# BigBird attention and a cosine router: turning, scores, values and row sums on 64x64 quarters of TensorE, with the router's logits taken along

## The chip, the cores and the metric

The kernel runs on one core of one Trainium2 chip. The metric is the device time of one execution in microseconds (us); less is better. The core has a matrix engine (TensorE, PE in the profile; its weight loads are listed as PEld), VectorE (DVE), ScalarE (ACT), GpSimd (POOL), and SyncE (SP), which issues most of the DMA transfers. Matrix products land in PSUM, which has eight banks of 512 float32 per partition; everything else is kept in SBUF.

## The reference

Block-sparse attention over 4 batches x 8 heads x 768 tokens x 64, followed by a mixture of 8 experts in which each token goes to one expert:

```python
scores = scale * np.matmul(q, k.transpose(0, 1, 3, 2))
scores = np.where(mask, scores, -1000000000.0)        # mask by blocks of 32 x 32
scores = scores - np.max(scores, axis=-1, keepdims=True)
attn = np.exp(scores)
attn = attn / (np.sum(attn, axis=-1, keepdims=True) + 1e-09)
out = np.matmul(attn, v)                              # then (B,H,S,D) -> x: (B*S, H*D)
...
xn = x / (np.linalg.norm(x, axis=-1, keepdims=True) + 1e-06)
en = expert_emb / (np.linalg.norm(expert_emb, axis=-1, keepdims=True) + 1e-06)
logits = xn @ en.T / tau
expert_idx = np.argmax(logits, axis=1)                # gate_w: the softmax there
h = np.maximum(x[mask] @ w1[e], 0.0)
out[mask] = gate_w[mask, None] * (h @ w2[e])
```

All inputs are float32.

## The kernel before

The attention (`attention_fast`, L527) goes over 16 pairs of heads. Of a pair, K and Q are loaded with tokens on partitions, three or so pairs ahead, and turned by TensorE so that the 2 x 64 head dimensions lie on the partitions (`turn_fast`, L248): four parts to a pair, each with three 128x128 transposes into one PSUM bank (L257) and one copy, of K by DVE (L261), of Q with the scale by ACT (L259).

The work of a pair is 12 units: two halves of the queries (384 each) times six chunks of 128 keys. `score_fast` (L264) makes the scores of a unit, keys on partitions, for both heads: first the mask, as a bf16 product of 24 block rows (L272; one product per head on 32 rows of the array), then K times Q with 64 rows of the array per head (L275), added onto it in PSUM; ACT takes the exponential of both heads at once (L278), without subtracting a maximum. `attend_fast` (L282) adds the unit's exponentials into `esum` on DVE (L291, L293) and multiplies them with V (L295): 128 rows of the array, 64 columns per head, added up in one PSUM bank over the six units of a half; after the sixth ACT copies the bank to `at` (L299).

`settle` (L303) finishes a half: three transposes bring `at` back to tokens on partitions (L313), six products of a column of ones sum `esum` over the keys (L317), and DVE divides (L320 to L323) and writes into `x`. After the eight halves of a batch, `route` squares the rows of `x` on ACT, takes the root on POOL (L354), transposes `x` again on TensorE, 24 times (L363), copies that on DVE (L365), and makes the logits with 48 matmuls of eight columns (L368). Then come some small DVE steps (L376 to L391) with the softmax and the argmax, and two products that rank the tokens within their expert (`rk`, L401 and L402). `dispatch` and `experts` follow when all four batches are routed. A second attention (`attention_exact`) stands in an If and isn't entered with these inputs.

Float32 products are two instructions each on TensorE (a load and a matmul twice); bf16 products and transposes are one. The loop of `attention_fast` (L545 to L557) gives the scores of the next unit, a part of a turn at four of the twelve units, the values of this unit, and settling one unit into the next half. Within that, the framework's scheduler sets the order of each engine's queue from its own plan, and the semaphores. PSUM: `big` has two buffers of two banks (scores, also the transposes of `x`), `acc` two of one bank (`av`), `small` two of one bank (turning, settling, logits, ranks).

Of the kernel before, what the change touches and what calls it, by code (L numbers as in the profile page):

```python
# [10 lines left out]
F32 = mybir.dt.float32  # L11
# [3 lines left out]
ALU = mybir.AluOpType  # L15
# [3 lines left out]
P = 128  # L19
# [22 lines left out]
class Net:  # L42
    pass

# [38 lines left out]
def build_mask(k):  # L83
# [39 lines left out]
    if not k.exact:  # L123
        k.kmask = k.const.tile([P, S], BF16, name="kmask")
        k.qmask = k.const.tile([P, S], BF16, name="qmask")
        for h in range(2):
            nc.vector.tensor_copy(out=k.kmask[32 * h:32 * h + NB, :], in_=krow)
            nc.scalar.copy(out=k.qmask[32 * h:32 * h + NB, :], in_=qr[0:NB, 0:S])
        return
# [10 lines left out]
def build_experts(k):  # L140
# [12 lines left out]
    tp = k.small.tile([P, 512], F32, name="tp", tag="small")  # L153
# [3 lines left out]
    nc.vector.tensor_copy(out=k.en, in_=tp[:, 0:ND * E].rearrange("p (c e) -> p c e", e=E))  # L157

# [67 lines left out]
def attend(k, u):  # L226
# [5 lines left out]
    if c == 0:  # L232
        k.av = k.small.tile([P, NC, D], F32, name="av", tag="small")
# [14 lines left out]
def turn_fast(k, g, part):  # L248

    nc = k.nc  # L250
    name, lo = ("k", "q")[part // 2], part % 2 * NQ
    if part == 0:
        k.turned[g] = {n: k.tp.tile([P, S], F32, name=f"{n}t", tag=f"{n}t") for n in ("k", "q")}
    src, dst = k.loaded[g]["kq".index(name)], k.turned[g][name]
    ps = k.small.tile([P, 512], F32, name="turn", tag="small")
    for c in range(NQ):
        nc.tensor.transpose(ps[:, c * P:(c + 1) * P], src[:, lo + c].rearrange("p h d -> p (h d)"), k.ident)  # L257
    if name == "q":
        nc.scalar.mul(out=dst[:, lo * P:lo * P + HALF], in_=ps[:, 0:HALF], mul=SCALE)  # L259
    else:  # L260
        nc.vector.tensor_copy(out=dst[:, lo * P:lo * P + HALF], in_=ps[:, 0:HALF])  # L261


def score_fast(k, u):  # L264
# [3 lines left out]
    kt, qt = k.turned[g]["k"], k.turned[g]["q"]  # L268
    ps = k.big.tile([P, 2, 512], F32, name="sc", tag="big")
    keys, queries = slice(kc * P, (kc + 1) * P), slice(qh * HALF, (qh + 1) * HALF)  # L270
# [11 lines left out]
def attend_fast(k, u):  # L282
# [3 lines left out]
    if kc == 0:  # L286
        k.av = k.acc.tile([P, 512], F32, name="av", tag="av")
# [6 lines left out]
    for h in range(2):  # L294
        nc.tensor.matmul(k.av[D * h:D * (h + 1), 0:HALF], lhsT=v[:, h, kc, :], rhs=e[:, h, :],  # L295
                         start=(kc == 0), stop=(kc == NC - 1))
    if kc == NC - 1:
        at = k.sp.tile([P, HALF], F32, name="at", tag="at")
        nc.scalar.copy(out=at, in_=k.av[:, 0:HALF])  # L299
        k.done[u // NC] = (at, k.esum)  # L300


def settle(k, w):  # L303
# [7 lines left out]
    ps = k.small.tile([P, 512], F32, name="back", tag="small")  # L311
# [8 lines left out]
    nc.vector.tensor_scalar(out=den, in0=ps[:, HALF:HALF + 2 * NQ], scalar1=1e-9, scalar2=None, op0=ALU.add)  # L320
    inv = k.sp.tile([P, NQ, 2], F32, name="inv", tag="inv")
    nc.vector.reciprocal(out=inv.rearrange("p t h -> p (t h)"), in_=den)
    nc.vector.tensor_tensor(  # L323
        out=k.x[b][:, qh * NQ:(qh + 1) * NQ, j * P:(j + 1) * P].rearrange("p t (h d) -> p t h d", h=2),
        in0=ps[:, 0:HALF].rearrange("p (t h d) -> p t h d", t=NQ, h=2),
        in1=inv.unsqueeze(3).broadcast_to([P, NQ, 2, D]), op=ALU.mult)


def count_good(k):
# [11 lines left out]
    ps = k.small.tile([P, 512], F32, name="good_ps", tag="small")  # L341
# [5 lines left out]
def route(k, b):  # L347
# [10 lines left out]
    lg = k.small.tile([P, NC, E], F32, name="lg", tag="small")  # L358
    for c2 in range(0, NC, 2):
        ps = k.big.tile([P, 2 * ND, P], F32, name="xt_ps", tag="big")  # L360
        for i in range(2 * ND):
            c, d = c2 + i // ND, i % ND
            nc.tensor.transpose(ps[:, i, :], x[:, c, d * P:(d + 1) * P], k.ident)  # L363
        xt = p.tile([P, 2 * ND, P], F32, name="xt")
        nc.vector.tensor_copy(out=xt, in_=ps)  # L365
        for c in (c2, c2 + 1):
            for d in range(ND):
                nc.tensor.matmul(lg[:, c, :], lhsT=xt[:, (c - c2) * ND + d, :], rhs=k.en[:, d, :],  # L368
                                 start=(d == 0), stop=(d == ND - 1))

# [156 lines left out]
def attention_fast(n, ctx):  # L527
# [14 lines left out]
    for part in range(4):  # L542
        turn_fast(n, 0, part)
    score_fast(n, 0)
    for u in range(units):  # L545
# [3 lines left out]
        if u + 1 < units:  # L549
            score_fast(n, u + 1)  # L550
# [136 lines left out]
```

## Time and profile before

| what | value |
|---|---|
| three runs | 997.63, 1002.25, 1003.86 us; median 1002.25 |
| profiled execution | 999.39 us, of which the span from its first to its last instruction is 997.6 |
| attention and routing | 20 to 547 us of the span |
| finding the slots, experts, tail | 547 to 998 us |
| granted clock of TensorE, mean over the span | 0.947 |

The profile records every instruction's start and duration on each engine, and what released it where it waited. Busy time on PE is the time in which at least one matmul is in the array, draining included; since matmuls overlap, the start of one group to the start of the next says more than the length of either. A load (PEld) belongs to a matmul and may run while an earlier matmul streams. The granted clock is a share of full speed, 1.00 for 2.4 GHz and 0.50 for 1.2 GHz.

### The profile page before, as it was taken

What the parts mean: (1) busy time and instruction counts of PE and PEld (TensorE: products, weight loads), DVE (VectorE), ACT (ScalarE), POOL (GpSimd) and SP (SyncE); (2) the same over time, 40 slices, a digit from 0 to 9 for tenths busy, and PEclk for the clock granted to TensorE, in tenths of its full rate; (3) what the DMA queues carried; (4) which work ended last, traced back from release to release, by engine and by line L of the source; (5) the groups of instructions that cost most, each with busy time, mean ns of one, the idle gap of its engine ahead of it and who ended that gap; (6) DMA issues with size and microseconds to landing.
All of it is one profiled execution on the core that took longest, in us unless ns stands there. A gap on an engine that the chain in (4) does not pass through costs nothing.

```text
span 997.6 us, 12554 instructions
## 1 busy us (share of the span) xinstructions
PE 942.3 (94%) x5230; PEld 542.6 (54%) x5230; DVE 298.0 (30%) x513; ACT 218.0 (22%) x340; POOL 73.1 (7%) x105
## 2 busy tenths in 40 slices
PE   5999999999999999999998489999999999999984
PEld 2344354344454434634446466766776776776662
DVE  2444443444434444334444511111111111111110
ACT  2434432433423444233342000000000000000000
POOL 1000000000010000100001100110110111111010
PEclk9999996999979999789996589999999999999997
DMA  7111112111221111020001299989889998998872
GB/s 174 30 34 49 48 32 80 48 44 37 48 79 33 48 49 32 17 79 1 1 1 42 102 400 407 401 311 342 306 314 329 311 326 316 330 321 314 289 280 77
DMA packets 105243, 161.69 MB, mean 162 GB/s; under 512 B 52620, under 2 KB 56716, under 8 KB 104662
## 3 DMA queue, kind: packets, MB, share of 16 engines
q1 hardware_dynamic: 100694, 146.84, 43.3%
q0 software_dynamic: 4480, 13.91, 3.5%
q8 instruction: 45, 0.74, 0.3%
q14 instruction: 24, 0.20, 0.1%
HBM read 148.14 MB, written 13.38 MB: 162 GB/s over the span
## 4 chain that ended last, share of the span: by engine, by line
PE 89%; issue 5%; DVE 2%; DMA 1%; SPq 1%; ACT 0%; POOL 0%; POOLq 0%; ACTq 0%
PE sc L275 18%; PE hp L510 18%; PE yp L518 17%; PE av L295 16%; PE sc L272 5%; PE back L317 4%; PE turn L257 3%; PE lg L368 3%; PE back L313 2%; PE xg_ps L501 1%; PE slot_ps L462 1%; PE xt_ps L363 1%; DMA out_dram<-y,slot 1%; SPq L173 1%; DVE xt L365 0%
## 5 line engine op out<-in xcount | busy, mean ns | idle before, releaser
L278 ACT ACTIVATE e<-sc 128x768 f32<-128x768 f32 x192 | 155.6, 810 | 287.3 <-PE sc L275 287.3
L510 PEld LDWEIGHTS hp<-xgt,w 128*128 128x128 f32 x1728 | 199.5, 192 | 25.4 <-issue 11.0
L510 PE MATMUL hp<-xgt,w 128*128 128x128 f32 x1728 | 204.2, 277 | 9.1 <-ACT h L513 4.9
L275 PE MATMUL sc<-qt,kt 64*128 64x384 f32 x768 | 192.4, 556 | 0.0
L518 PE MATMUL yp<-w,h 128*128 128x512 f32 x432 | 189.9, 592 | 0.0
L295 PE MATMUL av<-e,vld 128*64 128x384 f32 x768 | 173.1, 523 | 0.0
L293 DVE TENSOR_TENSOR esum<-esum,e 128x768 f32<-128x768 f32 x128 | 122.3, 956 | 105.9 <-ACT e L278 105.9
L518 PEld LDWEIGHTS yp<-w,h 128*128 128x128 f32 x432 | 80.0, 190 | 90.4 <-issue 90.4
L513 ACT ACTIVATE h<-hp 128x512 f32<-128x512 f32 x27 | 16.1, 597 | 412.7 <-PE hp L510 383.7
L295 PEld LDWEIGHTS av<-e,vld 128*64 128x64 f32 x768 | 39.2, 137 | 81.9 <-issue 63.4
L275 PEld LDWEIGHTS sc<-qt,kt 64*128 64x128 f32 x768 | 62.6, 191 | 35.9 <-issue 35.8
L272 PEld LDWEIGHTS <-kmask 24*128 24x128 bf16 x384 | 18.2, 91 | 102.3 <-issue 101.8
L520 DVE TENSOR_SCALAR y<-yp,xg 128x512 f32<-128x512 f32 x27 | 20.3, 750 | 158.6 <-PE yp L518 158.6
L514 DVE TENSOR_SCALAR h<-hp 128x512 f32<-128x512 f32 x27 | 18.7, 691 | 160.9 <-PE hp L510 160.9
L272 PE MATMUL sc<-qmask,kmask 24*128 24x384 bf16 x384 | 66.5, 340 | 0.0
L291 DVE TENSOR_TENSOR esum<-e 128x768 f32<-128x768 f32 x32 | 30.7, 958 | 110.6 <-ACT e L278 110.6
L521 POOL DMA_INDIRECT out_dram<-y,slot x27 | 27.5, 1017 | 352.9 <-DVE y L520 338.5
L317 PEld LDWEIGHTS back<-ones,esum 128*128 128x128 f32 x384 | 45.4, 192 | 0.0
L317 PE MATMUL back<-ones,esum 128*128 128x1 f32 x384 | 44.7, 243 | 0.0
L354 POOL TENSOR_TENSOR nrm<-nrm,half 128x6 f32<-128x6 f32 x4 | 5.3, 1330 | 485.3 <-ACT sq L353 485.3
L368 PEld LDWEIGHTS lg<-en,xt 128*128 128x128 f32 x192 | 29.4, 242 | 6.3 <-DVE xt L365 4.6
L486 POOL DMA_INDIRECT xg<-x_dram,slot x29 | 29.9, 1032 | 29.2 <-DVE slot L464 20.6
(124 smaller groups left out, 392.8 us busy)
## 6 DMA issues: line engine op xcount, KB each, us to landing
w<-in_moe_w_dram SPq DMA_DIRECT2D x58, 2048.0 KB, 9.4
x_dram<-x SPq DMA_DIRECT2D x4, 1539.0 KB, 6.1
kld<-in_k_dram SPq DMA_DIRECT2D x32, 192.0 KB, 3.0
qld<-in_q_dram SPq DMA_DIRECT2D x32, 192.0 KB, 3.2
vld<-in_v_dram SPq DMA_DIRECT2D x16, 384.0 KB, 3.2
xg<-x_dram,slot POOLq DMA_INDIRECT x29, 7.4
out_dram<-y,slot POOLq DMA_INDIRECT x27, 7.4
x_dram<-zero SPq DMA_DIRECT2D x1, 2.0 KB
```

Source lines behind the costliest of these rows:

```text
L257: nc.tensor.transpose(ps[:, c * P:(c + 1) * P], src[:, lo + c].rearrange("p h d -> p (h d)"), k.ident)
L272: nc.tensor.matmul(ps[:, h, 0:HALF], lhsT=k.kmask[32 * h:32 * h + NB, keys], rhs=k.qmask[32 * h:32 * h + NB, queries], start=True, stop=False)
L275: nc.tensor.matmul(ps[:, h, 0:HALF], lhsT=kt[D * h:D * (h + 1), keys], rhs=qt[D * h:D * (h + 1), queries], start=False, stop=True)
L278: nc.scalar.activation(e, ps[:, :, 0:HALF], ACT.Exp)
L291: nc.vector.tensor_tensor(out=k.esum, in0=k.first, in1=e, op=ALU.add)
L293: nc.vector.tensor_tensor(out=k.esum, in0=k.esum, in1=e, op=ALU.add)
L295: nc.tensor.matmul(k.av[D * h:D * (h + 1), 0:HALF], lhsT=v[:, h, kc, :], rhs=e[:, h, :], start=(kc == 0), stop=(kc == NC - 1))
L317: nc.tensor.matmul(ps[:, i:i + 1], lhsT=esum[:, h, t * P:(t + 1) * P], rhs=k.ones[:, 0:1], start=True, stop=True)
L368: nc.tensor.matmul(lg[:, c, :], lhsT=xt[:, (c - c2) * ND + d, :], rhs=k.en[:, d, :], start=(d == 0), stop=(d == ND - 1))
L486: nc.gpsimd.indirect_dma_start(out=x[:, :], out_offset=None, in_=k.x_dram[:, :], in_offset=bass.IndirectOffsetOnAxis(ap=k.slot[:, t:t + 1] ...
L510: nc.tensor.matmul(hp[:, f, :], lhsT=w1[:, d, f * P:(f + 1) * P], rhs=xt[:, d, :], start=(d == 0), stop=(d == ND - 1))
L518: nc.tensor.matmul(yp, lhsT=h[:, f, :], rhs=w2[:, f, :], start=(f == 0), stop=(f == NF - 1))
```

## The change

All products of the attention are cut so that each uses a 64x64 quarter of the array: 64 rows in, 64 columns out, and four such products, one for each quarter, follow one another. Products on different rows write different PSUM banks.

- The mask rows are padded from 24 to 64 per head with zeros (two fills on POOL). A unit's mask and scores are each four products: head by row half of the array, key half by column half.
- The values contract over 64 keys at a time, into two banks of `av`; `part` (ACT) copies one, and DVE adds the other to it to give `at`. `av` has one buffer of two banks instead of two of one.
- `turn_fast` has two parts instead of four, each for K and Q together: 24 products with the identity in place of transposes.
- `settle` turns `at` back with 12 products whose right side holds, beside the identity, the eight columns of the normalised expert embeddings for these 64 dimensions (`back`, built once in `build_experts`), and so gives each head's share of the logits; these go to `part`, and `route` sums them over the heads with one DVE step. The logits' transposes and products leave `route` (they stay for the exact path). The sums of `esum` are 24 products of one column.
- The loop gives scores two units ahead instead of one, settling before the values, and turning after them. `small` has one buffer of two banks instead of two of one.

```diff
+        nc.gpsimd.memset(k.kmask, 0.0)
+        nc.gpsimd.memset(k.qmask, 0.0)
...
+    k.back = k.const.tile([P, NPAIR, D + E], F32, name="back")
+    for h in range(2):
+        rows = slice(D * h, D * (h + 1))
+        nc.vector.tensor_copy(out=k.back[rows, :, 0:D],
+                              in_=k.ident[rows, rows].unsqueeze(1).broadcast_to([D, NPAIR, D]))
+        nc.vector.tensor_copy(out=k.back[rows, :, D:D + E], in_=k.en[rows])
...
 def turn_fast(k, g, part):
-    for c in range(NQ):
-        nc.tensor.transpose(ps[:, c * P:(c + 1) * P], src[:, lo + c].rearrange("p h d -> p (h d)"), k.ident)
+    for n in range(2):
+        src = k.loaded[g][n]
+        for c in range(NQ):
+            for r in range(2):
+                toks = slice(D * r, D * (r + 1))
+                for h in range(2):
+                    nc.tensor.matmul(ps[D * h:D * (h + 1), r, n, c, :], lhsT=src[toks, part * NQ + c, h, :],
+                                     rhs=k.ident[toks, toks], start=True, stop=True)
+    kt, qt = [t[:, chunks].rearrange("p c r t -> p r c t") for t in k.turned[g]]
+    nc.vector.tensor_copy(out=kt, in_=ps[:, :, 0])
+    nc.scalar.mul(out=qt, in_=ps[:, :, 1], mul=SCALE)
...
 def score_fast(k, u):
-    for h in range(2):
-        nc.tensor.matmul(ps[:, h, 0:HALF], lhsT=k.kmask[32 * h:32 * h + NB, keys],
-                         rhs=k.qmask[32 * h:32 * h + NB, queries], start=True, stop=False)
-    for h in range(2):
-        nc.tensor.matmul(ps[:, h, 0:HALF], lhsT=kt[D * h:D * (h + 1), keys], rhs=qt[D * h:D * (h + 1), queries],
-                         start=False, stop=True)
+    quarters = [(h, r, slice(kc * P + D * r, kc * P + D * (r + 1))) for r in range(2) for h in range(2)]
+    for rows, cols, first in ((k.kmask, k.qmask, True), (kt, qt, False)):
+        for h, r, keys in quarters:
+            nc.tensor.matmul(ps[D * r:D * (r + 1), h, 0:HALF], lhsT=rows[D * h:D * (h + 1), keys],
+                             rhs=cols[D * h:D * (h + 1), queries], start=first, stop=not first)
...
 def attend_fast(k, u):
-    for h in range(2):
-        nc.tensor.matmul(k.av[D * h:D * (h + 1), 0:HALF], lhsT=v[:, h, kc, :], rhs=e[:, h, :],
-                         start=(kc == 0), stop=(kc == NC - 1))
+    for r in range(2):
+        for h in range(2):
+            nc.tensor.matmul(k.av[D * h:D * (h + 1), r, 0:HALF], lhsT=v[D * r:D * (r + 1), h, kc, :],
+                             rhs=e[D * r:D * (r + 1), h, :], start=(kc == 0), stop=(kc == NC - 1))
     if kc == NC - 1:
+        part = k.sp.tile([P, HALF], F32, name="part", tag="part")
+        nc.scalar.copy(out=part, in_=k.av[:, 1, 0:HALF])
         at = k.sp.tile([P, HALF], F32, name="at", tag="at")
-        nc.scalar.copy(out=at, in_=k.av[:, 0:HALF])
+        nc.vector.tensor_tensor(out=at, in0=k.av[:, 0, 0:HALF], in1=part, op=ALU.add)
...
 def settle(k, w):
+    W = D + E
     for t in range(NQ):
-        nc.tensor.transpose(ps[:, t * P:(t + 1) * P], at[:, t * P:(t + 1) * P], k.ident)
-    for t in range(NQ):
         for h in range(2):
-            i = HALF + 2 * t + h
-            nc.tensor.matmul(ps[:, i:i + 1], lhsT=esum[:, h, t * P:(t + 1) * P], rhs=k.ones[:, 0:1],
-                             start=True, stop=True)
+            for s in range(2):
+                cols = slice(t * P + D * s, t * P + D * (s + 1))
+                nc.tensor.matmul(rows[D * s:D * (s + 1), t, h, :], lhsT=at[D * h:D * (h + 1), cols],
+                                 rhs=k.back[D * h:D * (h + 1), j, :], start=True, stop=True)
+    for t in range(NQ):
+        for h in range(2):
+            for r in range(2):
+                for s in range(2):
+                    cols = slice(t * P + D * s, t * P + D * (s + 1))
+                    nc.tensor.matmul(sums[D * s:D * (s + 1), t, h, r:r + 1], lhsT=esum[D * r:D * (r + 1), h, cols],
+                                     rhs=k.ones[D * r:D * (r + 1), 0:1], start=True, stop=True)
...
+    nc.vector.reduce_sum(out=den.rearrange("p (t h) -> p t h", t=NQ), in_=sums, axis=AX.X)
...
+    nc.vector.tensor_tensor(out=k.part[b][:, chunks, 2 * j:2 * j + 2, :], in0=rows[:, :, :, D:W],
+                            in1=inv.unsqueeze(3).broadcast_to([P, NQ, 2, E]), op=ALU.mult)
...
 def route(k, b):
+    lg = logits(k, x) if k.exact else l
+    if not k.exact:
+        nc.vector.reduce_sum(out=l, in_=k.part[b].rearrange("p c h e -> p c e h"), axis=AX.X)
...
 def attention_fast(n, ctx):
-    n.big, n.acc = pool("big_f", 2, space=PSUM), pool("acc", 2, space=PSUM)
+    n.big, n.acc = pool("big_f", 2, space=PSUM), pool("acc", 1, space=PSUM)
...
-        if u + 1 < units:
-            score_fast(n, u + 1)
-        if u % per in (2, 4, 8, 10) and g + 1 < pairs:
-            turn_fast(n, g + 1, (2, 4, 8, 10).index(u % per))
-        attend_fast(n, u)
         if u % NC == 1 and u > NC:
             settle(n, u // NC - 1)
             if (u - 1) % (per * NPAIR) == 0:
                 route(n, (u - 1) // (per * NPAIR) - 1)
+        attend_fast(n, u)
+        if u % per in (4, 9) and g + 1 < pairs:
+            turn_fast(n, g + 1, (4, 9).index(u % per))
+        if u + 2 < units:
+            score_fast(n, u + 2)
...
-    with tc.tile_pool(name="small", bufs=2, space=PSUM) as n.small:
+    with tc.tile_pool(name="small", bufs=1, space=PSUM) as n.small:
```

## Rows read from the trace of the kernel before

**Rows 1.** The page: busy time, clock in 40 slices, chain by engine.
```profile
PE 942.3 (94%) x5230; PEld 542.6 (54%) x5230; DVE 298.0 (30%) x513; ACT 218.0 (22%) x340; POOL 73.1 (7%) x105
...
PEclk9999996999979999789996589999999999999997
...
PE 89%; issue 5%; DVE 2%; DMA 1%; SPq 1%; ACT 0%; POOL 0%; POOLq 0%; ACTq 0%
```

**Rows 2.** Busy time by stretches (us, then each engine, PEclk, DMA share, GB/s).
```profile
134.30:168.10 33.80, 33.36 (x159) 18.21 (x157) 12.45 (x27) 7.38 (x14) 3.25 (x7) 0.75 0.22 73
150.40:167.50 17.10, 17.10 (x50) 7.38 (x51) 5.86 (x17) 2.94 (x5) 1.90 (x6) 0.50 0.32 115
168.10:266.90 98.80, 98.80 (x569) 41.09 (x567) 42.72 (x62) 42.03 (x63) 0.00 (x0) 1.00 0.16 40
547.10:997.60 450.50, 411.32 (x2322) 300.89 (x2321) 70.64 (x133) 16.12 (x27) 57.39 (x56) 0.95 0.84 305
```

**Rows 3.** Timeline of PE within one half: start, us, what, how many.
```profile
226.38 0.34 PE L272 MATMUL sc<-qmask,kmask 24*128 24x384 bf16 x2
226.64 0.92 PE L275 MATMUL sc<-qt,kt 64*128 64x384 f32 x4
227.49 0.87 PE L295 MATMUL av<-e,vld 128*64 128x384 f32 x4
228.28 0.55 PE L313 MATMUL back<-ident,at 128*128 128x128 f32 x3
228.67 1.40 PE L317 MATMUL back<-ones,esum 128*128 128x1 f32 x12
230.00 0.34 PE L272 MATMUL sc<-qmask,kmask 24*128 24x384 bf16 x2
...
231.11 0.55 PE L257 MATMUL turn<-ident,qld 128*128 128x128 f32 x3
231.58 0.87 PE L295 MATMUL av<-e,vld 128*64 128x384 f32 x4
```

**Rows 4.** Chain in order of time; timeline of loads; groups of 168.1 to 266.9.
```profile
588.29 6.87 PE yp L518 x16
...
225.58 0.20 PEld L295 LDWEIGHTS av<-e,vld 128*64 128x64 f32 x4 [0.55 <-ACT at L299]
228.56 1.42 PEld L317 LDWEIGHTS back<-ones,esum 128*128 128x128 f32 x12
...
L317 PEld LDWEIGHTS back<-ones,esum 128*128 128x128 f32 x84 | 9.9, 192 | 0.0
L295 PEld LDWEIGHTS av<-e,vld 128*64 128x64 f32 x168 | 8.3, 134 | 17.6 <-issue 13.8 <-ACT at L299 3.8
```

**Rows 5.** Groups of one route (138 to 171 us) on PE: busy us, mean ns.
```profile
L368 PE MATMUL lg<-en,xt 128*128 128x8 f32 x48 | 6.7, 275 | 0.4 <-DVE xt L365 0.4
L363 PE MATMUL xt_ps<-ident,x 128*128 128x128 f32 x24 | 3.0, 276 | 0.0
```

**Rows 6.** Groups of 168.1 to 266.9 on ACT and DVE: busy us, mean ns, idle before.
```profile
L278 ACT ACTIVATE e<-sc 128x768 f32<-128x768 f32 x42 | 34.0, 810 | 54.1 <-PE sc L275 54.1
L293 DVE TENSOR_TENSOR esum<-esum,e 128x768 f32<-128x768 f32 x28 | 26.8, 956 | 24.3 <-ACT e L278 24.3
...
L323 DVE TENSOR_TENSOR x<-back,inv 128x384 f32<-128x384 f32 x7 | 3.9, 558 | 0.2
...
L299 ACT COPY at<-av 128x384 f32<-128x384 f32 x7 | 3.4, 480 | 0.2 <-PE av L295 0.2
```

**Rows 7.** Timeline of all engines, last settling and last route.
```profile
529.02 1.40 PE L317 MATMUL back<-ones,esum 128*128 128x1 f32 x12
...
534.67 1.32 POOL L354 TENSOR_TENSOR nrm<-nrm,half 128x6 f32<-128x6 f32 x1 [113.68 <-ACT sq L353]
...
543.52 0.21 DVE L376 TENSOR_TENSOR l<-lg,nrm 128x48 f32<-128x48 f32 x1 [4.97 <-PE lg L368]
...
547.14 0.56 PE L411 MATMUL cp<-seen,ones 128*128 128x8 f32 x2
```

More of the change, by code (lines that the diff above doesn't have):

```diff
@@ L43, with two_banks @@
     pass
+def two_banks(k, name):
+    return k.small.tile([P, 2, 512], F32, name=name, tag="small")
 def iota(k, name, shape, pattern, base=0, mult=0):
@@ L232, in attend @@
     if c == 0:
[L233 removed]
+        k.av = two_banks(k, "av")[:, 0, 0:NC * D].rearrange("p (c e) -> p c e", e=D)
     for kc in range(NC):
@@ L250, in turn_fast @@
     nc = k.nc
-    name, lo = ("k", "q")[part // 2], part % 2 * NQ
     if part == 0:
-        k.turned[g] = {n: k.tp.tile([P, S], F32, name=f"{n}t", tag=f"{n}t") for n in ("k", "q")}
-    src, dst = k.loaded[g]["kq".index(name)], k.turned[g][name]
-    ps = k.small.tile([P, 512], F32, name="turn", tag="small")
-    for c in range(NQ):
-        nc.tensor.transpose(ps[:, c * P:(c + 1) * P], src[:, lo + c].rearrange("p h d -> p (h d)"), k.ident)
[L258 to L261, printed above, removed]
+        k.turned[g] = [k.tp.tile([P, NC, 2, D], F32, name=f"{n}t", tag=f"{n}t") for n in ("k", "q")]
+    ps = two_banks(k, "turn")[:, :, 0:2 * NQ * D].rearrange("p r (n c t) -> p r n c t", n=2, t=D)
+    chunks = slice(part * NQ, (part + 1) * NQ)
+    for n in range(2):
[9 more added lines that the diff above has]
+    nc.scalar.mul(out=qt, in_=ps[:, :, 1], mul=SCALE)
 def score_fast(k, u):
@@ L310, in settle @@
         k.x[b] = k.xp.tile([P, NC, XW], F32, name="x", tag="x")
-    ps = k.small.tile([P, 512], F32, name="back", tag="small")
-    for t in range(NQ):
-        nc.tensor.transpose(ps[:, t * P:(t + 1) * P], at[:, t * P:(t + 1) * P], k.ident)
+        k.part[b] = k.xp.tile([P, NC, H, E], F32, name="part", tag="part")
+    ps = two_banks(k, "back")
+    W = D + E
+    rows = ps[:, :, 0:NQ * W].rearrange("p h (t w) -> p t h w", t=NQ)
+    sums = ps[:, :, NQ * W:NQ * W + 2 * NQ].rearrange("p r (t h) -> p t h r", t=NQ)
@@ L321, in settle @@
+    nc.vector.tensor_scalar(out=den, in0=den, scalar1=1e-9, scalar2=None, op0=ALU.add)
     inv = k.sp.tile([P, NQ, 2], F32, name="inv", tag="inv")
     nc.vector.reciprocal(out=inv.rearrange("p t h -> p (t h)"), in_=den)
+    chunks = slice(qh * NQ, (qh + 1) * NQ)
     nc.vector.tensor_tensor(
[L324 to L326 removed]
+        out=k.x[b][:, chunks, j * P:(j + 1) * P].rearrange("p t (h d) -> p t h d", h=2),
+        in0=rows[:, :, :, 0:D], in1=inv.unsqueeze(3).broadcast_to([P, NQ, 2, D]), op=ALU.mult)
@@ L344, in count_good, with logits @@
     nc.vector.tensor_copy(out=k.good, in_=ps[:, 0:1])
-def route(k, b):
-    nc, p, x = k.nc, k.rp, k.x[b]
-    nrm = p.tile([P, NC], F32, name="nrm")
-    for c in range(NC):
-        sq = p.tile([P, DM], F32, name="sq")
-        nc.scalar.activation(sq, x[:, c, 0:DM], ACT.Square, accum_out=nrm[:, c:c + 1])
-    nc.gpsimd.tensor_tensor(out=nrm, in0=nrm, in1=k.half, op=ALU.pow)
-    nc.vector.tensor_scalar(out=nrm, in0=nrm, scalar1=1e-6, scalar2=None, op0=ALU.add)
-    nc.vector.reciprocal(out=nrm, in_=nrm)
-    lg = k.small.tile([P, NC, E], F32, name="lg", tag="small")
+def logits(k, x):
+    nc, p = k.nc, k.rp
+    lg = two_banks(k, "lg")[:, 0, 0:NC * E].rearrange("p (c e) -> p c e", e=E)
     for c2 in range(0, NC, 2):
@@ L369, in route @@
                                  start=(d == 0), stop=(d == ND - 1))
+    return lg
+def route(k, b):
+    nc, p, x = k.nc, k.rp, k.x[b]
+    nrm = p.tile([P, NC], F32, name="nrm")
+    for c in range(NC):
+        sq = p.tile([P, DM], F32, name="sq")
+        nc.scalar.activation(sq, x[:, c, 0:DM], ACT.Square, accum_out=nrm[:, c:c + 1])
+    nc.gpsimd.tensor_tensor(out=nrm, in0=nrm, in1=k.half, op=ALU.pow)
+    nc.vector.tensor_scalar(out=nrm, in0=nrm, scalar1=1e-6, scalar2=None, op0=ALU.add)
+    nc.vector.reciprocal(out=nrm, in_=nrm)
     def wide(t):
@@ L541, in attention_fast @@
         build_experts(n)
-    for part in range(4):
+    for part in range(2):
         turn_fast(n, 0, part)
     score_fast(n, 0)
+    score_fast(n, 1)
     for u in range(units):
@@ L628 @@
     n.loaded, n.vs, n.es, n.ets, n.sums, n.x, n.fetched = {}, {}, {}, {}, {}, {}, {}
-    n.turned, n.done = {}, {}
+    n.turned, n.done, n.part = {}, {}, {}
     n.exact = False
@@ L646 @@
         n.exact = True
-        with tc.tile_pool(name="small_x", bufs=2, space=PSUM) as n.small:
+        with tc.tile_pool(name="small_x", bufs=1, space=PSUM) as n.small:
             with ExitStack() as attn:
```

21 lines of the change are left out of this document (10 added, 11 removed).

## The prediction

> **What bounds the kernel now.** I read the page's busy shares first: TensorE (PE) is busy for 94% of the span, no other engine for more than a third, and the chain that ended last is 89% PE [rows 1]. The clock line shows that PE mostly runs at its full clock, with dips. Second, the busy time by stretches [rows 2]: from 168.10 to 266.90 us, seven query halves with no routing between them, PE is busy without a gap, so a half costs 98.80 / 7 = 14.114 us of PE, and there are 32 of them. A stretch with one routing in it (134.30 to 168.10, the same one half and a route) takes 33.80, so a route costs 19.7 us, and there are three inside attention: 59 us. In the 17.1 us behind a route the granted clock is 0.50 [rows 2], the 1.2 GHz level: part of the route's price is that everything there runs at half speed. The fourth route lies bare at the end of attention [rows 7]. The 450.50 us behind it (slots, experts, tail) have no edit worth a microsecond in them.
>
> Third, the timeline of one half on PE [rows 3]. A unit runs L272 at 226.38, L275 at 226.64, L295 at 227.49, next group at 228.28: 0.26 + 0.85 + 0.79 = 1.90 us. The transposes of `at` start at 228.28, the column sums of `esum` at 228.67, and the next unit starts at 230.00: settling costs 1.72. A turn takes from 231.11 to 231.58, 0.47, two to a half. Sum: 6 x 1.90 + 1.72 + 0.94 = 14.1, the half of [rows 2].
>
> Fourth, what these groups would cost if only streaming counted. 16 fp32 instructions of 512 columns take 6.87 us [rows 4], 0.429 each, so one of 384 columns takes 0.322. A float32 product is two instructions. L275 has four, on two halves of the rows; in 0.85 us they can only have run two abreast (four in series would be 1.29): 0.644 is streaming and 0.21 is not. L295 has four on two halves of the columns: 0.644 and 0.15. The bf16 mask has one instruction to a product where float32 has two; I estimate its streaming at half of 0.322, 0.161 (it cannot be over 0.26), and 0.10 that is not. So 0.46 us in each unit are spent where one group ends and another, with another split of the array, begins: weights are loaded with nothing streaming, and the old products drain. That is what the change can take away.
>
> **The change, part by part.** *Units.* Mask, scores and values all become four products on 64x64 quarters. The work per array cell is unchanged, so with four abreast the streaming is 0.161 + 0.644 + 0.644 = 1.45; no group has another split than its neighbours any more, so loads can run ahead. I take 1.48 (0.03 for three group starts). Bounds: 1.45, and 1.90 if the seams stay.
>
> *Turning.* A half's two turns of three transposes (0.94) become one `turn_fast` of 24 products with the identity, 48 pairs of load and matmul. *Settling.* Three transposes and six sums (1.72) become 12 products of 72 columns and 24 of one column, 24 + 48 pairs. The trace has no such pair. The nearest rows: L317 starts 12 loads of 128 columns in 1.42 us, one lasting 0.192, so one per (1.42 - 0.192) / 11 = 0.112 us; L295's four loads of 64 columns lie within 0.20 us though one lasts 0.134 [rows 4], so two load abreast, and half the columns is half of 0.112: 56 ns for two, 28 ns per pair. Four abreast would be 14. Bounds 14 and 112; I take 28, since it is the row with the same number of columns on a split array. Turning: 48 x 28 = 1.34; settling: 72 x 28 = 2.02. (The 72 columns stream in 60 ns, four abreast 15: hidden under 28.)
>
> A rule bears on this. The Trainium skill, "TensorEngine Tiling (Array Packing)", Performance Considerations, Instruction Overhead, speaks against cutting products that are already small: every matmul has about 60 cycles of overhead, so one column costs what 60 do. At 2.4 GHz that is 25 ns (an estimate from that page) and would make the 120 pairs 3.0 us, a total near 880; it would exclude the 14.
>
> Half after: 6 x 1.48 + 1.34 + 2.02 = 12.24, saving 14.11 - 12.24 = 1.87; times 32: 60 us.
>
> *Routes.* The logits leave PE: 24 transposes (L363) and 48 matmuls of eight columns (L368) to a route [rows 5], replaced by the eight extra columns of `back`, which cost no pair. The rest of the chain stays: squares on ACT, the power on POOL, seven small DVE steps, two `rk` products that PE must run in its order. At the end of attention the steps from `l` to the next product take 543.52 to 547.14, 3.6 us [rows 7]; I take 4 us per inner route, as if PE waited for all of that. Bounds: 1 (other units fill it) and the 19.7 of before (PE waits, the clock falls again). Saving 59 - 12 = 47 us, and it needs the low clock to go: the clock falls where PE has long runs of eight-column products, and these leave.
>
> *The bare last route.* Settling ends at 529.02 + 1.40 = 530.42; the power ends at 534.67 + 1.32 = 535.99, waiting for no logits; then two small steps (0.4, estimated from the 0.2 of their like) and 3.6: 540.0 in place of 547.14. Saving 7.
>
> *What is added elsewhere.* Per half ACT copies `part` where it copied `at` (0.48); DVE gets an add like L323 (0.56) and two small steps [rows 6]. ACT: 6 x 0.81 + 0.48 + 0.48 = 5.8 of 12.2 us; DVE: 5 x 0.96 + 3 x 0.56 (`at`, `kt`, `x`) + about 0.8 = 7.3. Both hide behind PE. The set-up's two fills on POOL and four copies on DVE come six units before the first settling needs them: nothing, or about 1 us without that cover. The dummy rows of the mask (64 in place of 24) add no column: nothing.
>
> *The accumulator has one buffer instead of two.* The first value product of a half must wait until `part` (0.48) and the add (0.56) have emptied it; behind it on PE's queue stand the next scores and settling. Cover: the score group issued between, 0.81. Exposed: 1.04 - 0.81 = 0.23. I take 0.2 x 32 = 6 us; bounds 0 and 1.05 x 32 = 34. `small` also has one buffer, but its users (settling at units 1 and 7, turning at 4 and 9) lie two units, 3 us, apart: nothing, or a part of 1 us per use if DVE lags.
>
> **The sum.** The profiled execution took 999.39 us (span 997.6 and 1.8 around it), inside the three runs (997.63 to 1003.86), 2.9 below their median. 999.4 - 60 - 47 - 7 + 6 = 891 us. With the low ends (14 ns, 1 us a route, no accumulator wait): half 6 x 1.48 + 120 x 0.014 = 10.56, so 999.4 - 114 - 56 - 7 = 822.
>
> **Rivals.** *Two abreast, not four (slower).* No row shows four tiles streaming at once; rows and columns each show two. If a quarter product still shares the array with one other, a unit is 0.32 + 1.29 + 1.29 = 2.90, a half 20.8, +213 us: 999.4 + 213 - 48 = 1164. It decides at 5.8 / k = 2.04 us a unit (where a half costs 14.11 + (47 + 7 - 6) / 32 = 15.6), so at fewer than 2.8 abreast. For it: nothing in the trace; against it: L275 and L295 split each dimension freely. 0.07.
>
> *The queue hands out pairs slowly.* If L317's 112 ns were no matter of 128 columns but of the queue, a half of 240 pairs (20 to a unit) would be 26.9 us: 1361. Against: L295's loads lie closer. It decides at (15.6 - 8.9) / 120 = 56 ns a small pair; at 45 ns the time is 957. Full price 0.02, the part way 0.08.
>
> *Routes keep their price:* PE waits out the chain and the clock drops: 891 + 47 = 938. For it: the chain's ACT, POOL and DVE work is all still there, and PE takes its queue in order. 0.13.
>
> *The accumulator's emptying becomes the bound:* 34 in place of 6: 919. The Trainium skill, "TensorEngine Tiling (Array Packing)", PSUM Bottleneck, warns that tiling quickens TensorE but not the emptying of PSUM, which may then bound. By busy time the trace leaves room (7.3 of 12.2), so only this wait is left to it. 0.08.
>
> *My forecast:* four abreast, seams gone, small pairs near 28 ns, routes cheap: 891, with its own range 825 to 920. 0.62.
>
> **How the numbers follow.** The range reaches from the low ends to the routes' rival and half of the slow queue: 830 to 962; outside lie the two slow rivals, the upper half of slow pairs, and a little below. More than 1% (10 us, about what runs that scatter by 6 us can tell) faster: 0.88; within 1%: 0.03, the part-way queue near 56 ns; slower: 0.09.
>
> **What would show it.** A half without routing (from one `part` copy to the next) of 12.2 us; units of 1.48 with no idle PE; scores and values each as eight matmuls in about 0.65 us; turning 1.3 and settling 2.0 us; no 0.50 clock between 150 and the end of attention; route stretches of 16 us; attention over near 440 us. Wrong if value matmuls wait on `at` for over 0.5 us, if the eight matmuls of a group start in twos, or if the stretch of single-column sums is over 3 us.

## The result, and the profile after

The changed kernel takes 891.8 us (median of four executions, 890.98 to 892.23); the kernel before, beside it on the same chip, 1003.1. The ratio is 0.890, with a 95% interval of 0.887 to 0.893. The profiled execution took 890.98 us, its span 889.2, where that of before had 999.39 and 997.6: 108.4 us less. The forecast was 891. It will be seen that this is not because its terms were right. Among all executions timed here two stood far off, one of the kernel before at 1540.74 us and one of `rank_late` at 2827.88, and the figures leave both out.

The page of after (busy time, clock in 40 slices, chain by engine), beside [rows 1]:

```profile
PE 780.1 (88%) x10030; PEld 507.1 (57%) x10030; DVE 315.2 (35%) x605; ACT 215.1 (24%) x340; POOL 74.7 (8%) x107
...
PEclk9999989999899997999659999999999999999997
...
PE 72%; ACT 8%; DVE 7%; issue 7%; DMA 2%; POOL 2%; SPq 1%; POOLq 0%; ACTq 0%; DVEq 0%
```

PE is busy for 162 us less, with nearly twice the instructions. The chain that ended last is PE's for 72% of it, not 89%: ACT and DVE now have 15% together, where they had 2%. So PE waits for them at places, and the clock line still dips three times within the attention (slices 6, 11 and 16).

Where the 108.4 us lie is read from the copies that empty the accumulator, one to a half, of which the first and the last bound the attention; `cp` is the first product of the dispatch. First both copies of before (timeline of ACT: start, us, engine, line, what, and in brackets the idle time ahead of it with what ended it):

```profile
35.41 0.48 ACT L299 COPY at<-av 128x384 f32<-128x384 f32 x1
...
528.11 0.48 ACT L299 COPY at<-av 128x384 f32<-128x384 f32 x1 [1.15 <-PE av L295]
```

Then both of after, and its `cp` (timeline):

```profile
33.65 0.48 ACT L315 COPY part<-av 128x384 f32<-128x384 f32 x1
...
426.77 0.48 ACT L315 COPY part<-av 128x384 f32<-128x384 f32 x1 [0.99 <-PE av L311]
...
438.85 0.57 PE L449 MATMUL cp<-seen,ones 128*128 128x8 f32 x2 [0.39 <-DVE pick L441]
```

A route's price is what the two halves at a batch's end take over two halves elsewhere.

| stretch | before, us | after, us | saved | forecast |
|---|---|---|---|---|
| start to the first copy | 35.4 | 33.6 | 1.8 | 0 |
| first to last copy, without routes | 435.0 | 357.3 | 77.7 | 54 |
| the three routes in it | 57.7 | 35.9 | 21.8 | 47 |
| last copy to `cp` | 19.0 | 12.1 | 6.9 | 7 |
| `cp` to the end | 450.5 | 450.4 | 0.1 | 0 |
| sum | 997.6 | 889.2 | 108.4 | 108 |

The halves gave 24 us more than was forecast and the routes 25 less. That is the thing to explain.

**A half.** Six halves of after without routing (138.30 to 207.60, busy time by stretches, columns as in [rows 2]):

```profile
138.30:207.60 69.30, 65.43 (x1448) 36.50 (x1440) 41.61 (x72) 33.85 (x50) 0.00 (x0) 1.00 0.22 54
```

The timeline of after, from a unit to a turn, the end of a half, and settling (PE, with ACT and DVE where they empty the accumulator):

```profile
200.36 0.82 PE L290 MATMUL sc<-qt,kt 64*64 64x384 f32 x8
...
201.00 0.82 PE L311 MATMUL av<-e,vld 64*64 64x384 f32 x8
...
201.65 0.34 PE L290 MATMUL sc<-qmask,kmask 64*64 64x384 bf16 x4
...
201.81 0.82 PE L290 MATMUL sc<-qt,kt 64*64 64x384 f32 x8
...
204.55 0.53 PE L273 MATMUL turn<-ident,kld 64*64 64x64 f32 x24
...
205.25 0.34 PE L290 MATMUL sc<-qmask,kmask 64*64 64x384 bf16 x4
...
206.06 0.82 PE L311 MATMUL av<-e,vld 64*64 64x384 f32 x8
...
206.52 0.49 ACT L277 ACTIVATE qt<-turn 128x384 f32<-128x384 f32 x1 [1.49 <-DVE kt L276]
...
206.91 0.81 ACT L293 ACTIVATE e<-sc 128x768 f32<-128x768 f32 x1
207.60 0.48 ACT L315 COPY part<-av 128x384 f32<-128x384 f32 x1
...
208.11 0.56 DVE L317 TENSOR_TENSOR at<-av,part 128x384 f32<-128x384 f32 x1 [1.63 <-ACT part L315]
...
208.73 0.88 PE L311 MATMUL av<-e,vld 64*64 64x384 f32 x8 [1.04 <-DVE at L317]
...
210.23 0.56 PE L338 MATMUL back<-back,at 64*64 64x72 f32 x24
...
210.61 0.82 PE L345 MATMUL back<-ones,esum 64*64 64x1 f32 x48
...
211.28 0.86 PE L311 MATMUL av<-e,vld 64*64 64x384 f32 x8
```

The waits of PE in after, the three largest (what waits, for what; us in total, times, the longest):

```profile
PE av L311 <- DVE at L317: 20.8, 31, 1.0
PE rk L439 <- DVE gate L428: 15.6, 4, 7.3
PE av L311 <- ACT e L293: 12.7, 8, 1.8
```

A half takes 69.30 / 6 = 11.55 us (14.114 before). A unit: 200.36 to 201.81, 1.45. The turn: 204.55 to 205.25, 0.70. Settling: 210.23 to 211.28, 1.05. Together 6 x 1.45 + 0.70 + 1.05 = 10.45; the other 1.10 is for the most part the wait for the accumulator. Here it is 1.22: the values begin at 206.06 and, with nothing in the way, would again at 206.06 + 1.45 = 207.51, but begin at 208.73. That is the end of a half in which the turn stands one unit before the last. In the other half of a pair it stands two before, and there the wait is shorter (timeline of PE):

```profile
194.91 0.88 PE L311 MATMUL av<-e,vld 64*64 64x384 f32 x8
...
196.97 0.88 PE L311 MATMUL av<-e,vld 64*64 64x384 f32 x8 [0.39 <-DVE at L317]
```

194.91 + 1.45 = 196.36, so 0.61 are lost. The two kinds alternate, 0.92 in the mean; the remaining 0.18 is spread over the groups around the wait, among them values that wait for an exponential which ACT begins late. (The waits view counts 1.0 and 0.4 in turn, the time with nothing in the array.)

### The profile page after: what moved, and what is told of

Its sections match the earlier page's. It is cut to its first block, busy times and chain, and to the rows that moved or that the text cites. A ratio compares the mean times of both kernels' runs of the same rounds, so it can differ in the third digit from the quotient of the medians.

```text
span 889.2 us, 22238 instructions
## 1 busy us (share of the span) xinstructions
PE 780.1 (88%) x10030; PEld 507.1 (57%) x10030; DVE 315.2 (35%) x605; ACT 215.1 (24%) x340; POOL 74.7 (8%) x107
## 3 DMA queue, kind: packets, MB, share of 16 engines
q8 instruction: 82, 1.34, 0.6%
## 4 chain that ended last, share of the span: by engine, by line
PE 72%; ACT 8%; DVE 7%; issue 7%; DMA 2%; POOL 2%; SPq 1%; POOLq 0%; ACTq 0%; DVEq 0%
PE hp L548 19%; PE yp L556 19%; PE sc L290 13%; PE av L311 12%; ACT e L293 4%; PE turn L273 2%; DVE at L317 2%; PE back L345 2%; ACT sq L401 2%; DVE esum L308 2%; ACT part L315 2%; PE slot_ps L500 1%; PE back L338 1%; PE xg_ps L539 1%; DMA xg<-x_dram,slot 1%
## 5 line engine op out<-in xcount | busy, mean ns | idle before, releaser
L311 PE MATMUL av<-e,vld 64*64 64x384 f32 x1536 | 172.4, 500 | 33.7 <-DVE at L317 20.8
L290 PE MATMUL sc<-qt,kt 64*64 64x384 f32 x1536 | 165.9, 490 | 0.0
L311 PEld LDWEIGHTS av<-e,vld 64*64 64x64 f32 x1536 | 53.7, 135 | 105.4 <-DVE at L317 41.5
L290 PEld LDWEIGHTS sc<-qt,kt 64*64 64x64 f32 x1536 | 61.5, 135 | 33.5 <-issue 30.9
L290 PE MATMUL sc<-qmask,kmask 64*64 64x384 bf16 x768 | 69.0, 328 | 0.0
L290 PEld LDWEIGHTS <-kmask 64*64 64x64 bf16 x768 | 25.5, 109 | 26.7 <-issue 26.1
L541 DVE COPY xgt<-xg_ps 128x512 f32<-128x512 f32 x27 | 18.5, 687 | 42.4 <-PE xg_ps L539 42.4
L317 DVE TENSOR_TENSOR at<-av,part 128x384 f32<-128x384 f32 x32 | 17.8, 558 | 33.5 <-ACT part L315 33.5
L273 PEld LDWEIGHTS turn<-ident,kld 64*64 64x64 f32 x768 | 20.1, 145 | 14.5 <-issue 10.8
## 6 DMA issues: line engine op xcount, KB each, us to landing
w<-in_moe_w_dram SPq DMA_DIRECT2D x58, 2048.0 KB, 10.7
```

Source lines behind the costliest of these rows:

```text
L273: nc.tensor.matmul(ps[D * h:D * (h + 1), r, n, c, :], lhsT=src[toks, part * NQ + c, h, :], rhs=k.ident[toks, toks], start=True, stop=True)
L290: nc.tensor.matmul(ps[D * r:D * (r + 1), h, 0:HALF], lhsT=rows[D * h:D * (h + 1), keys], rhs=cols[D * h:D * (h + 1), queries], start=first ...
L311: nc.tensor.matmul(k.av[D * h:D * (h + 1), r, 0:HALF], lhsT=v[D * r:D * (r + 1), h, kc, :], rhs=e[D * r:D * (r + 1), h, :], start=(kc == 0 ...
L317: nc.vector.tensor_tensor(out=at, in0=k.av[:, 0, 0:HALF], in1=part, op=ALU.add)
```

## The experiments

Two theories stand for the halves and the routes. For the halves: PE loses 1.1 us in each because it waits until ACT and DVE have emptied the accumulator. For the routes: PE waits in turn for ACT, DVE and POOL, since each engine takes its queue in order, and the low clock follows the waits. Their rivals are in the expectations. Times stand against the 891.8 of the changed kernel; each run had the kernel before beside it on its chip (1002.0 to 1002.7).

### The accumulator

*Make the emptying longer* (`slow_copy`): ACT copies `part` once more before the add, about 0.5 us.

```diff
+        nc.scalar.copy(out=part2, in_=part)
-        nc.vector.tensor_tensor(out=at, in0=k.av[:, 0, 0:HALF], in1=part, op=ALU.add)
+        nc.vector.tensor_tensor(out=at, in0=k.av[:, 0, 0:HALF], in1=part2, op=ALU.add)
```

> Changed kernel with the suspected wait made longer: ACT copies part once more (0.48 and a hand-over) before DVE adds. Theory A: each half is 0.5 to 0.55 us longer, 31 x 0.52 = 16 us slower, near 907. Rival B: within 3 us of 891.

909.7 us (ratio 0.909, 0.905 to 0.913): 18 more. The halves went from 11.35 and 11.75, which alternate, to 11.89 and 12.29, each 0.54 longer. All of what was added came out at the end; nothing covers it.

*Make it shorter, by two copies at once* (`two_copies`): DVE copies bank 0 while ACT copies bank 1, and adds afterwards from SBUF.

```diff
-        nc.vector.tensor_tensor(out=at, in0=k.av[:, 0, 0:HALF], in1=part, op=ALU.add)
+        nc.vector.tensor_copy(out=at0, in_=k.av[:, 0, 0:HALF])
+        nc.vector.tensor_tensor(out=at, in0=at0, in1=part, op=ALU.add)
```

> Changed kernel, but both banks of av are emptied at the same time (ACT copies one, DVE the other, DVE adds the two in SBUF afterwards). Theory A, the single accumulator buffer costs 1.1 us of each half because the copy (0.48) and the add (0.56) stand in series before the first value product of the next half: the add leaves the wait, about 0.5 us x 31 = 16 us faster than the changed kernel, near 876. Rival B, the halves take 11.55 us for another reason (weights loaded without cover, the order of the queues) and the wait only stands where PE would idle anyway: within 3 us of 891.

893.0 us (0.892, 0.889 to 0.896): nothing gained. The halves are as before, 11.35 and 11.75, and its timeline says why:

```profile
207.91 0.48 ACT L315 COPY part<-av 128x384 f32<-128x384 f32 x1
...
208.43 0.56 DVE L318 COPY at<-av 128x384 f32<-128x384 f32 x1 [1.63 <-ACT part L315]
209.02 0.56 DVE L319 TENSOR_TENSOR at<-at,part 128x384 f32<-128x384 f32 x1
209.04 0.88 PE L311 MATMUL av<-e,vld 64*64 64x384 f32 x8 [1.04 <-DVE at L318]
```

DVE's copy reads another bank and nothing that ACT writes, and yet it waits until ACT is done: the two banks are one tile, and two engines that read one tile are put one behind the other. So this run didn't test what it was made for.

*The same with two tiles* (`two_tiles`): `av` becomes two tiles of one bank.

```diff
-        k.av = k.acc.tile([P, 2, 512], F32, name="av", tag="av")
+        k.av = [k.acc.tile([P, 512], F32, name=f"av{r}", tag=f"av{r}") for r in range(2)]
```

> The copies of e1_two_copies again, but av is two tiles of one bank each, so that nothing orders DVE's copy behind ACT's (in e1 DVE's copy stood waiting for ACT's part 32 times, so the wait e1 was to shorten was as long as before). Theory A: the accumulator is empty when the later copy ends, 0.5 to 0.6 us earlier than now, and each of 31 halves is that much shorter: 16 to 18 us faster than the changed kernel, near 875, halves of 11.0 in place of 11.55. Rival B: within 3 us of 891.

875.4 us (0.875, 0.872 to 0.877): 16.4 less. Its timeline at the end of a half:

```profile
211.99 0.56 DVE L318 COPY at<-av 128x384 f32<-128x384 f32 x1
212.05 0.48 ACT L315 COPY part<-av 128x384 f32<-128x384 f32 x1
...
212.65 0.88 PE L311 MATMUL av<-e,vld 64*64 64x384 f32 x8
212.66 0.56 DVE L319 TENSOR_TENSOR at<-at,part 128x384 f32<-128x384 f32 x1
```

Now both copies run together and the next values start when they end, while the add is still to come. The halves are 10.77 and 11.22, 11.00 in the mean, so 0.55 us of the 1.10 are gone, and 31 x 0.55 = 17 is the gain.

*Do without the quarters in the values* (`values_halves`): 128 rows of the array and 64 columns, two buffers of one bank, no `part`, as before the change. It tells what a change of the array's split costs, and what the accumulator's second buffer is worth.

```diff
-    for r in range(2):
-        for h in range(2):
-            nc.tensor.matmul(k.av[D * h:D * (h + 1), r, 0:HALF], lhsT=v[D * r:D * (r + 1), h, kc, :],
-                             rhs=e[D * r:D * (r + 1), h, :], start=(kc == 0), stop=(kc == NC - 1))
+    for h in range(2):
+        nc.tensor.matmul(k.av[D * h:D * (h + 1), 0:HALF], lhsT=v[:, h, kc, :], rhs=e[:, h, :],
+                         start=(kc == 0), stop=(kc == NC - 1))
```

> Changed kernel with the values alone put back as they were before: 128 keys, two products on halves of the columns, one bank, two buffers, no part and no add. Theory S, what the units gained are the seams between groups that split the array differently: two seams come back in each unit (0.15 behind the values, 0.1 to 0.2 behind the scores), the unit goes from 1.45 to about 1.75, the wait for the accumulator (1.1 us a half) goes: half 6 x 1.75 + 0.70 + 1.05 = 12.25, 32 x 0.7 = 22 us slower than the changed kernel, near 914. Rival Q, quarters cost nothing at their borders and the gain is from the order of the loop and from the logits: half 10.5, 34 us faster, near 857.

898.3 us (0.898, 0.895 to 0.901), 6.5 more. PE in two of its units:

```profile
205.19 0.36 PE L290 MATMUL sc<-qmask,kmask 64*64 64x384 bf16 x4
205.38 0.81 PE L290 MATMUL sc<-qt,kt 64*64 64x384 f32 x8
206.12 0.87 PE L310 MATMUL av<-e,vld 128*64 128x384 f32 x4
...
206.92 0.36 PE L290 MATMUL sc<-qmask,kmask 64*64 64x384 bf16 x4
```

A unit takes 1.73 us, 0.28 more for the two places where the split changes, 0.14 each in the mean, with the same streaming. That is what the seams cost. The total is less than their 54 us (6 x 0.28 x 32) because the wait for the accumulator is gone: a half is 12.12 in the mean, 6 x 1.73 + 0.70 + 1.05 = 12.13, with nothing over. The routes also cost 8.6 us here, not 12: 54 - 35 - 10 = 9, against 6.5 measured.

### The routes

*Make the logits on TensorE again* (`logits_back`): the one part of the change that touches the routes, undone.

```diff
-    lg = logits(k, x) if k.exact else l
-    if not k.exact:
-        nc.vector.reduce_sum(out=l, in_=k.part[b].rearrange("p c h e -> p c e h"), axis=AX.X)
+    lg = logits(k, x)
```

> Changed kernel whose route makes the logits on TensorE again (24 transposes, 48 products of eight columns; the eight extra columns of back are still computed and not used). The forecast's view, all of what a route lost was the logits: 3 x 8 us or more and 7 at the end, near 925 to 930. Rival: in an inner route PE stands at the ranking products for 4 us and at the exponentials for 3.5 anyway, so half of the 8 us fills idle time: 3 x 4 + 7 = 19, near 910.

930.8 us (0.929, 0.926 to 0.933), 39 more: 10.7 for each of the three routes and 7 for the last one. So of the 108 us the logits' leaving is 39. The rest is what the quarters gave together with the loop's new order and the single buffers that came with them; no run kept the quarters and put the old order back. The low clock lasts 17.1 us in the first route, as it did before [rows 2] (this kernel, busy time by stretches):

```profile
126.10:143.20 17.10, 15.46 (x84) 10.71 (x86) 4.23 (x15) 1.75 (x3) 1.20 (x6) 0.50 0.22 92
```

The same of the changed kernel:

```profile
125.90:136.10 10.20, 6.23 (x65) 4.20 (x69) 4.81 (x15) 1.75 (x3) 1.96 (x6) 0.50 0.38 156
```

The logits stretch the low clock, but it comes without them, for 10.2 us. What sets PE idle ahead of it is seen in the changed kernel's first route (timeline):

```profile
122.08 0.63 ACT L401 ACTIVATE sq<-x 128x512 f32<-128x512 f32 x1 [2.13 <-DVE x L353]
...
123.93 0.79 ACT L293 ACTIVATE e<-sc 128x768 f32<-128x768 f32 x1
124.11 1.35 POOL L402 TENSOR_TENSOR nrm<-nrm,half 128x6 f32<-128x6 f32 x1 [109.70 <-ACT sq L401]
...
127.61 0.24 ACT L426 ACTIVATE l<-l 128x48 f32<-128x48 f32 x1 [2.89 <-DVE pick L420]
...
128.44 0.63 PE L439 MATMUL rk<-oh,before 128*128 128x48 f32 x2 [2.81 <-DVE gate L428]
...
130.50 0.66 PE L440 MATMUL rk<-seen,ones 128*128 128x48 f32 x2 [1.42 <-POOL seen L437]
```

The exponential at 123.93 stands behind three squares on ACT; the values wait for it (1.8 us, the third line of the waits above). Then ACT stands at L426 for DVE's chain, and PE at `rk` for DVE and for POOL: 2.81 + 1.42. That is 6.0 us in which PE has nothing, and then it works at half speed until 136.1: 6.23 us busy there, of which by estimate half, 3.1, is the clock's. Of this route's 12.25 us the half ahead has 1.9, for the squares of the first three chunks; 6.0 and 3.1 are accounted for here, and 1.2 I could not place.

*Take the squares out* (`no_squares`; the norm is set to 1, so the routing's normalisation is left out).

```diff
-        nc.scalar.activation(sq, x[:, c, 0:DM], ACT.Square, accum_out=nrm[:, c:c + 1])
+    nc.vector.memset(nrm, 1.0)
```

> Changed kernel without the 24 squared norms of the tokens on ACT: the norm is taken as 1 (so the logits are not normalised; the choice of expert is the same, the gate is not). Theory D: PE's waits for an exponential in the half before and in the half of a route go (1.7 + 1.8 us a batch), the ranking products wait less, and the last route is 2 us shorter: 4 x 3.5 + 2 + up to 6, near 870. Theory C alone: only what the chain to the ranking products is shorter, 3 x 2.4 + 2, near 882.

879.6 us (0.879, 0.875 to 0.882): 12 less. The half ahead of a route goes from 13.26 to 11.35; the half with it still takes 21.9, 21.8 and 19.2, and `rk` and the low clock stay. The three routes still cost 27.8 us of 35.9, and the other 4 us were gained at the bare end. So the squares are a part of a route's price, under a quarter, and not its cause.

*Rank six units later* (`rank_late`): the two `rk` products and their DVE steps move to the next half, by which time their operands are long there.

```diff
+def rank(k, b):
+    got = p.tile([P, NC, E], F32, name="got")
...
+            if (u - 1) % (per * NPAIR) == NC and u > per * NPAIR:
+                rank(n, (u - 1) // (per * NPAIR) - 1)
```

> Changed kernel with the two ranking products of each route issued one half (six units) later than the route. Theory C, an inner route still costs 12 us because PE stands at the ranking products until DVE and POOL are through (2.8 + 1.3 us) and then runs 7 to 10 us at the 1.2 GHz level: both go, some 7 us a route, 21 us in all, near 870, and no stretch of granted clock 0.50 is left between 30 us and the end of attention. Rival D, the price is ACT's squares ahead of the exponentials (about 1.8 us before and in each route half): at most 5 us faster, and the low clock stays.

884.5 us (0.883, 0.878 to 0.888): 7 less, a third of what theory C expected. Its waits of PE, the line that grew:

```profile
PE av L311 <- ACT e L293: 19.2, 12, 2.1
```

The wait for `rk` in the routes is gone (15.6 - 7.3 of the last one, which is bare), and 6.5 us of it came back as waits for exponentials that stand behind the squares and L426 on ACT. Nor did the low clock go as theory C had it: it lasts 3.4 us once in the first route and twice in the second, and is gone from the third. That third route still costs 8.3 us (its four halves take 13.26 + 15.95 + 13.52 + 11.75, four elsewhere 46.2), so the greater part of the price is the waits and not the clock.

*Spread the squares, one to a unit, and tie gate and rank to later exponentials* (`tied_route`), so that the framework's plan can't move them forward.

```diff
+        if u > all_of - 5 and (turn in {all_of - 4, all_of - 3, all_of - 2}):
+            square(n, u // all_of, turn - (all_of - 4), u)
+        if u > all_of and turn in {2, 3, 4}:
+            square(n, u // all_of - 1, NQ + turn - 2, u)
+        if u > all_of and turn == 5:
+            route(n, u // all_of - 1)
+        if u > all_of and turn == 11:
+            rank(n, u // all_of - 1, u)
```

> Changed kernel in which the squares come one to a unit, and the gate and the two ranking products half a batch-quarter later (unit 11), each held there by an operand that takes zero times the exponentials of that unit; two small DVE steps a route and one a square more. Theory E, an inner route costs 12 us because three in-order queues stand still in turn (ACT at the squares and at the gate, PE at the ranking products) and the clock then drops: all three go, a route costs 3 us or less, 27 us in all, near 864, and no 0.50 clock from 30 us to the end of attention. Rival: the stalls only move to the next place where a queue waits for the chain (as in e3, 7 us faster): 880 to 886.

886.9 us (0.887, 0.883 to 0.890), 5 less, as the rival had it; the low clock too is still in every route, for 3.4, 6.8 and 3.4 us. The wait has moved on from ACT and sits in DVE's queue (timeline of its first route):

```profile
127.80 0.17 DVE L418 TENSOR_SCALAR nrm<-nrm 128x6 f32<-128x6 f32 x1 [1.45 <-POOL nrm L417]
...
130.66 0.55 DVE L276 COPY kt<-turn 128x384 f32<-128x384 f32 x1
131.24 0.49 ACT L277 ACTIVATE qt<-turn 128x384 f32<-128x384 f32 x1 [4.20 <-DVE kt L276]
...
132.32 0.48 ACT L315 COPY part<-av 128x384 f32<-128x384 f32 x1
132.84 0.56 DVE L317 TENSOR_TENSOR at<-av,part 128x384 f32<-128x384 f32 x1 [1.63 <-ACT part L315]
133.45 1.56 PE L311 MATMUL av<-e,vld 64*64 64x384 f32 x8 [4.26 <-DVE at L317]
```

The route's chain waits on DVE for POOL's power; the turn's copy of K stands behind the chain; ACT's copy of Q stands behind that (one tile again); the exponentials and `part` behind Q; and PE behind `part`.

*Both together, with the chain's first step tied as well* (`both_tied`): two accumulator tiles, and the route called two units later, its first DVE step tied to the exponentials of that unit, so that K's copy goes first.

```diff
-        if u > all_of and turn == 5:
-            route(n, u // all_of - 1)
+        if u > all_of and turn == 7:
+            route(n, u // all_of - 1, u)
...
+        nc.vector.scalar_tensor_tensor(out=tied, in0=k.es[u][:, 0, 0:NC], scalar=0.0, in1=nrm,
+                                       op0=ALU.mult, op1=ALU.add)
```

> The accumulator as two one-bank tiles (as in the run before that did so), the route's squares one to a unit, its first VectorE step tied to the exponentials of the eighth unit, gate and rank products to those of the twelfth. Theory (the route's excess is in-order queues: whatever waits on another engine holds what is queued behind it): with the wait for POOL's power gone from VectorE's queue, the turn's copy of K is no longer held, a route half comes down from 22 to 14 us or less and the low clock goes, so 3 x 8 = 24 us less than the 875 of two tiles alone: 848 to 858. Rival (the plan of the framework moves the wait to another instruction again, as in the tied route before): 870, the sum of the two earlier gains of 16 and 5 us.

853.7 us (0.851, 0.849 to 0.854), in the middle of what the theory gave. (The tie and the two units' delay came together; no run tells them apart.) Its page (busy time, clock):

```profile
PE 775.9 (91%) x10030; PEld 538.2 (63%) x10030; DVE 334.4 (39%) x667; ACT 217.4 (25%) x340; POOL 76.2 (9%) x107
...
PEclk9999999999999999997579999999999999999997
```

And the largest wait of PE in it (waits):

```profile
PE av L311 <- ACT e L293: 9.5, 14, 0.9
```

The four halves around the first route take 12.34, 12.95, 12.05 and 12.47, against 43.98 for four undisturbed: 5.8 us for the route, 5.0 and 4.8 for the next two, near the 4 that was forecast. The wait for the accumulator's add has left the list, and the clock doesn't fall between 24.0 and 392.6 us, though nothing was taken out of TensorE's work. So the low clock inside the attention went with the waits.

*Two tiles and the late ranks* (`two_late`), to see whether gains add.

> The accumulator as two one-bank tiles, and the rank products six units later, squares and gate left where they are. If the two gains add, 892 - 16 - 7 = 868. If the wait for the rank products was only exchanged for one that the quicker accumulator lays bare, 875, that of two tiles alone.

866.1 us (0.865, 0.862 to 0.869): 25.7 less, 16.4 + 7.3 = 23.7 by the two alone. They add. The low clock is left in one route, for 3.4 us.

## Why the forecast held, and where its terms didn't

**Four abreast: right.** The scores' eight instructions take 0.82 us with the draining, where one lasts 0.49. The first four start within 0.04 us (timeline 201.80 to 201.84):

```profile
201.81 0.50 PE L290 MATMUL sc<-qt,kt 64*64 64x384 f32 x4
```

The next four start 0.32 later. The unit is 1.45 (1.48 forecast), and both slow rivals (two abreast, a slow queue) fall. 6 x 0.03 = 0.2 us a half.

**The small pairs: mis-sized by half.** Turning and settling are 120 pairs of load and product; 28 ns each was taken, from a row of loads on a split array in pairs. Measured: 0.70 / 48 and 1.05 / 72, both 14.6 ns, which is the lower bound that the prediction gave and did not take. That is the rate of loads four abreast, as the products are: a half has 1.34 + 2.02 - 0.70 - 1.05 = 1.61 us less than forecast, 51 us over the kernel. The page that the prediction weighed (the Trainium skill, "TensorEngine Tiling (Array Packing)", Instruction Overhead) gives about 60 cycles a matmul, by estimate 25 ns, and was said to exclude 14. The trace decides against it for products on four quarters: a round of four pairs takes 58 ns, not 100.

**The accumulator: the step that failed.** Forecast 0.2 us a half, measured 1.10 with what hangs on it: 0.9 x 32 = 29 us. The two durations were right (0.48 and 0.56), and so was the cover, 0.81 by the next scores. What was left out stands ahead of the copy. In every half the last products have to drain (206.06 + 0.82 = 206.88, while PE has gone on since 206.70), and the hand-overs take their part: so 0.2 becomes 0.61. In every second half ACT then begins, at 206.91, an exponential that its queue has ahead of `part`, which so starts at 207.60: another 0.6, and the 1.22. That exponential's scores were there at 205.41 + 0.82 = 206.23. ACT came to it late because it stood at its copy of Q until DVE had copied K (the 1.49 at 206.52); both copies read one PSUM tile, as the two copies of `av` did. No run gave K and Q a tile each, so what that would bring isn't shown. The rival "the accumulator's emptying becomes the bound" was the right account at its price of 34 us, and had 0.08. The prediction's own sign of error, values that wait on `at` for over 0.5 us, is there with 1.0 in every second half. With an emptying 0.54 longer, and with one that gave 0.55 back, the time moved by just that.

The Trainium skill, "TensorEngine Tiling (Array Packing)", PSUM Bottleneck, had warned that the emptying may come to bound. The prediction put it aside by busy time, and the busy time was as it said: DVE is busy for 41.61 of 69.30 us. It isn't the throughput of the emptying that bounds but its delay, with one buffer: a distinction that busy shares can't show.

**The routes: the second step that failed.** Forecast 4 us each, measured 11.5 to 12.3: 24 us in all. "PE waits for all of the chain" was costed from the bare chain at the end [rows 7], 3.6 us. Inside attention the chain doesn't run bare: its steps stand in three queues among the units' work, and each step that waits holds that work up, which holds up PE at other places (exponentials behind squares, `rk`). The prediction's test was no clock of 0.50 before the end of attention; the three dips of 10.2, 6.8 and 10.2 us show its reason wrong too. The low clock was put down to the eight-column products; in the runs it came without them and went when the waits went. By the third route of `rank_late`, 8.3 us with no low clock, the waits are the larger part.

**The bare last route: right** (7 forecast, 6.9 measured), as was nothing for set-up and dispatch.

So: -51 (pairs) + 29 (accumulator and what hangs on it) + 24 (routes) - 6 (units) = -4 against the forecast, and the ends of the attention, where a half isn't a whole one, give that back: 32 x (14.11 - 11.55) = 82, and 77.7 measured. That the total came out at 891 is luck: terms that are off by 51 and 53 cancelled.

## What to carry to other kernels

When a buffer is halved to make room, cost the wait from the moment that the last product has drained to the moment that the buffer is free, with all that the emptying engine has queued ahead of the copy, not with the copy's own duration; and give two engines that are to empty it together a tile each. A side chain over several in-order engines is priced by what stands behind each of its waits, and moving one wait mostly uncovers the next: in these runs the route became cheap only when the squares, the first DVE step and the ranks had all been moved, though whether it needed all three wasn't tested. Check each term of a sum against the trace even where the total is right.

## What the runs showed of the hardware

Products on the four quarters run beside one another (a group of eight with 384 columns takes 0.65 us from start to start, where one lasts 0.49), and pairs of load and product with 1 to 72 columns take 14.6 ns each, though one load lasts 133 to 145 ns. A change of the array's split costs 0.14 us in the mean (the unit of 1.73 with two of them against 1.45 with none). Reads of one PSUM tile by ACT and DVE are put one behind the other by the framework's semaphores, even in different banks; as two tiles they overlap by 0.5 us. The granted clock of the changed kernel fell to 0.50 for 6.8 to 10.2 us in each route, from the middle of waits of PE that sum to some 6 us there; in the kernel whose longest such wait is 0.9 us it stayed at 1.00 through all three.
